# The 47-point part of a transform in front of a feed-forward layer: even and odd sums in six of eight batches

## The chip, the core and the metric

The kernel runs on one core of one Trainium2 chip. The metric is the device time of one execution in microseconds (us); the time before is the median of three runs. A profile of one more execution shows every instruction on the five engines: TensorE (PE, with its weight loads on a line of their own, PEld), VectorE (DVE), ScalarE (ACT), GpSimd (POOL) and SyncE (SP), whose queue issues the transfers (DMA) here.

## The reference

```python
def _attn_ref(x):                      # x: 8 x 3008 x 256, float32
    X = np.fft.fft(x, axis=1)
    X = np.fft.fft(X, axis=2)
    return X.real.astype(np.float32)

def _moe_ref(x, w_in, w_out):          # 24064 tokens, 256 -> 2048 -> 256
    h = x @ w_in
    beta = 1.0
    neg = h <= -beta
    pos = h >= beta
    mid = ~neg & ~pos
    g = np.where(pos, h, np.where(neg, 0.0, (h + beta) ** 2 / (4.0 * beta)))
    return (g @ w_out).astype(np.float32)
```

The real part of a two-dimensional Fourier transform of every batch, and behind it a feed-forward layer over all 8 x 3008 rows of it. The input's layout is changed on the host before the launch and the output's after it; the arithmetic is on the chip.

## The kernel before

**The transform.** 3008 is 64 x 47, so a row number splits into a part of 64 (a) and a part of 47 (b), and the transform along it into a 47-point part (stage 1) and a 64-point part (stage 2). The host sends each element beside the one at the opposite row and column, and the kernel adds the two (`fold_x`, line 137, on POOL): the real part needs no more than this sum. Of the 47 frequencies 24 are computed, since the rest follow by symmetry. The transform along the 256 columns is multiplied into `w_in` once, so the layer's first product takes the rows from stage 2 as they are. One column (number 128, called Nyquist) has a path of its own: a small product (`nyquist`, line 312), a detour of its rows through DRAM, and a term that DVE adds later.

**Stage 1** (`stage1`, line 275) has eight pieces for each batch, one for each tile of 8 x 2 columns. The tile `x` is 128 rows by 2 by 384 values; the first index of 2 is the element and its opposite, and the 384 rows of the product are 8 columns of 47 values, filled up with zeros and cut into three blocks of 128. POOL adds the halves into a tile `y` of 384 columns (line 142; three buffers), which lets the x tile go. PE then multiplies three blocks as weights with a block-diagonal constant of cosines and sines, 144, 192 and 144 columns wide (line 287), all in float32, which takes two instructions for each product. ACT copies the result from the PSUM bank to the tile `z` in four parts of 64 x 192 (line 307). The first piece of a batch also has a difference `yd` (line 148) and one product for the Nyquist column (line 299), with two copies of 64 x 24. All pieces share the one PSUM bank `fft`.

**Stage 2** (`stage2`, line 340) has six pieces of four products of 128 columns (line 350); ACT and DVE split each result into a high and a low half (`pqh`, `pql`).

**The layer.** The work is cut into 384 units: 8 batches, 3 chunks of rows (482, 512 and 512), 16 parts of the 2048 hidden values; batch 0 goes over its chunks twice with 8 parts each. A unit has a first product of 6 PE instructions (`gemm1`, line 396), then DVE's `us` and the two halves of `h` (lines 409, 411, 412), ACT's two steps (417, 418), DVE's larger-of (429, both its inputs in SBUF), ACT's rounding to `gh` (430) and POOL's two low halves `gl` (436), and a second product of 12 PE instructions (`gemm2`, line 448), which runs four units later (`LAG`). Of `uv` there are three PSUM banks, of `h` and `a` three buffers, of `gh` and `gl` four.

**What sets the order.** The start (`LOADS`, `START`) is written out by hand. From there on the program emits, for each unit, its first product, its activation, the weight steps of `STEPS` and the transform pieces due at that unit, and then the second product of the unit four earlier. `PLAN` gives the units of a batch's 15 pieces relative to 48 units before the batch's own, `SECOND_PLAN` those of batch 1. A planner then orders each engine's instructions by readiness in its own simulated time, with program order as priority; the first product of a transform piece is pinned behind what was emitted on PE before it (`pinned`). Within an engine's queue the order is then fixed. Loads of x wait in SP's queue for one of four buffers called `xt`, which the raw weights use too in the first part of the run.

Of the kernel before, what the change touches and what calls it, by code (L numbers as in the profile page):

```python
# [13 lines left out]
ALU = mybir.AluOpType  # L14
# [3 lines left out]

NB, S, D, FF = 8, 3008, 256, 2048
NA, NBB, NC = 64, 47, 24
P = 128
XC = 8
GPC = 4
KT = 3
XW = KT * P
CH = 512
# [12 lines left out]
BM = np.cumsum([0] + [hi - lo for lo, hi in SPANS])  # L41


def _constants():
# [13 lines left out]
    parts = [bm, rm]  # L58
# [59 lines left out]


@with_exitstack  # L120
def fft_ffn_kernel(ctx: ExitStack, tc: tile.TileContext, x, cst, w_in, w_out, out):
    nc = tc.nc

    wts = ctx.enter_context(tc.tile_pool(name="wts", bufs=1))
# [4 lines left out]
    xt, yt, zt, nyb, pq, rows = {}, {}, {}, {}, {}, {}  # L129

    def load_x(b, q):
        tag, bufs = ("xt", 4) if b or q < 4 else ("gl", 4) if q < 7 else ("o", 2)
        t = sb.tile([P, 2, XW], F32, tag=tag, name=f"x_{b}_{q}", bufs=bufs)
        nc.sync.dma_start(t, x[b, q])
        xt[b, q] = t

    def fold_x(b, q):

        t = xt.pop((b, q))
        if b or q:  # L140
            y = sb.tile([P, XW], F32, tag="y", name=f"y_{b}_{q}", bufs=3) if b else t[:, 0]
            nc.gpsimd.tensor_tensor(y, t[:, 0], t[:, 1], op=ALU.add)  # L142
            yt[b, q] = [y]
        else:
            yt[b, q] = [t[:, 0], t[:, 1]]
        if q == 0:
            y = sb.tile([P, NA], F32, tag="yd", name=f"yd_{b}", bufs=1)
            nc.gpsimd.tensor_tensor(y, t[:, 0, :NA], t[:, 1, :NA], op=ALU.subtract)
            yt[b, "d"] = y

    cs = wts.tile([P, _OFF[2]], F32, name="cs")
    nc.sync.dma_start(cs, cst[:, : _OFF[2]])
    bm, rm = (cs[:, _OFF[i] : _OFF[i + 1]] for i in range(2))
    cm = sb.tile([P, _OFF[6] - _OFF[2]], F32, tag="nyb", name="cm", bufs=4)
# [8 lines left out]
    nc.vector.memset(half, 0.5)  # L163

    def load_cm():
        nc.sync.dma_start(cm, cst[:, _OFF[2] :])

    early = [0]

# [98 lines left out]
    def first_delta():  # L268
# [3 lines left out]
            nc.tensor.matmul(pt[:, i], t[:, i * P : (i + 1) * P], half[:1].to_broadcast([1, NA]), start=True, stop=True)  # L272
        nc.scalar.activation(delta[:, :4], pt[:, :, 0], AF.Copy, scale=2.0)

    def stage1(b, q):
        for p in range(q, min(q + 2, XC)):
            if (b, p) in xt and (b, p) not in yt:
                fold_x(b, p)
        if q == 0:
            zt[b] = sb.tile([P, NC, P + 1], F32, tag="z", name=f"z_{b}", bufs=1)  # L280
        z, y = zt[b], yt[b, q]
        bank = fft_bank(b, f"s1_{b}_{q}")
        pt = bank[:, : 8 * 2 * NC]
        for k, (lo, hi) in enumerate(SPANS):
            for j, part in enumerate(y):
                at = k, j
                mm = nc.tensor.matmul(  # L287
                    pt[:, lo:hi],
                    part[:, k * P : (k + 1) * P],
                    bm[:, BM[k] : BM[k + 1]],  # L290
                    start=at == (0, 0),
                    stop=at == (KT - 1, len(y) - 1),
                    skip_group_check=True,
                )
                if at == (0, 0):
                    pinned(b, mm)
        if q == 0:
            pd = bank[:NA, 8 * 2 * NC : 9 * 2 * NC]
            nc.tensor.matmul(pd, yt[b, "d"], bm[:, : 2 * NC], start=True, stop=True)
        for h in range(2):  # L300
            for m in range(2):
                src = pt[h * NA : (h + 1) * NA].rearrange("p (t m c) -> p m c t", t=8, m=2)[:, m]
                dst = z[m * NA : (m + 1) * NA, :, (2 * q + h) * 8 : (2 * q + h + 1) * 8]
                if b == 0 and q in VECTOR_COPIES:
                    nc.vector.tensor_copy(dst, src)
                else:
                    nc.scalar.activation(dst, src, AF.Copy)  # L307
        if q == 0:
            for m in range(2):
                nc.scalar.activation(z[m * NA : (m + 1) * NA, :, P], pd[:, m * NC : (m + 1) * NC], AF.Copy)  # L310

    def nyquist(b):
        pt = fft_bank(b, f"ny_{b}")
# [43 lines left out]
    def pinned(b, matmul):  # L357

        if b:
            tc.keep_in_program_order(matmul)  # L360

    def fft_pieces(b):
        pieces = []
        for q in range(XC):
            pieces.append(lambda q=q: stage1(b, q))
# [126 lines left out]
    def fill(n):  # L492
# [105 lines left out]
```

## Time and profile before

| | |
|---|---|
| median of 3 runs | 1733.8 us (1732.95 to 1735.46) |
| the profiled execution's own time | 1732.59 us |
| its span, first to last instruction | 1730.8 us |
| granted TensorE clock | 0.998 |
| PE busy | 1716.5 us |
| DVE busy | 1383.6 us |
| ACT busy | 1359.8 us |
| POOL busy | 1204.8 us |

Some 1.8 us of the execution lie outside the span. Busy times are sums over the span: an engine that is busy for 99% of it may set the time, one at 70% may still set it somewhere. In the rows of the views an engine, a line of the kernel and an operation come first, then output and inputs by the program's names; `x6` at the end of a row is a count. In the chain and the timeline the first two numbers are the start and the length in us from the span's start, and what stands in brackets at the end is the idle time before and what ended it. Matmuls overlap in their ends, so the time that one adds to a row of them is read from starts, not from its own length.

### The profile page before, as it was taken

What the parts mean: (1) busy time and instruction counts of PE and PEld (TensorE: products, weight loads), DVE (VectorE), ACT (ScalarE), POOL (GpSimd) and SP (SyncE); (2) the same over time, 40 slices, a digit from 0 to 9 for tenths busy, and PEclk for the clock granted to TensorE, in tenths of its full rate; (3) what the DMA queues carried; (4) which work ended last, traced back from release to release, by engine and by line L of the source; (5) the groups of instructions that cost most, each with busy time, mean ns of one, the idle gap of its engine ahead of it and who ended that gap; (6) DMA issues with size and microseconds to landing.
All of it is one profiled execution on the core that took longest, in us unless ns stands there. A gap on an engine that the chain in (4) does not pass through costs nothing.

```text
span 1730.8 us, 21504 instructions
## 1 busy us (share of the span) xinstructions
PE 1716.5 (99%) x7784; PEld 1412.5 (82%) x7784; DVE 1383.6 (80%) x1682; ACT 1359.8 (79%) x1593; POOL 1204.8 (70%) x857
## 2 busy tenths in 40 slices
PE   8999999999999999999999999999999999999999
PEld 5877888888888888888888888888888888888877
DVE  6987888777888777877788878887788787888887
ACT  6888877888778887778877887778877788777776
POOL 3767876777667776677757686667866666766775
PEclk9999999999999999999999999999999999999999
DMA  6123220111001110010100111001100001000000
GB/s 232 36 71 123 102 77 25 46 32 62 1 25 51 37 53 20 5 60 29 52 25 10 51 37 43 25 10 57 47 28 26 9 24 43 1 25 24 1 25 25
DMA packets 33456, 72.44 MB, mean 42 GB/s; under 512 B 4547, under 2 KB 9667, under 8 KB 33350
## 3 DMA queue, kind: packets, MB, share of 16 engines
q1 hardware_dynamic: 33350, 71.07, 12.2%
q8 instruction: 61, 1.00, 0.2%
q14 instruction: 45, 0.37, 0.1%
HBM read 43.25 MB, written 27.81 MB: 41 GB/s over the span
## 4 chain that ended last, share of the span: by engine, by line
PE 92%; ACT 2%; POOL 2%; DVE 2%; issue 1%; DMA 1%; ACTq 0%; POOLq 0%
PE acc L468 57%; PE uv L400 29%; PE s L287 3%; PE s L350 2%; POOL gl L436 2%; DVE h L429 1%; ACT gh L430 1%; ACT a L418 1%; ACT a L417 0%; PE wps L249 0%; DMA nyr<-nyt 0%; PE warm L494 0%; DMA nyb<-nyr 0%; ACT z L307 0%; DVE h L412 0%
## 5 line engine op out<-in xcount | busy, mean ns | idle before, releaser
L436 POOL TENSOR_TENSOR gl<-h,gh 128x512 fp32r<-128x512 f32 (+1 forms) x765 | 1100.7, 1462 | 483.0 <-ACT gh L430 433.2
L429 DVE SCALAR_TENSOR_TENSOR h<-a,h 128x1024 f32<-128x1024 f32 (+1 forms) x385 | 560.9, 1458 | 184.1 <-ACT a L418 182.4
L430 ACT ACTIVATE gh<-h 128x1024 fp32r<-128x1024 f32 (+1 forms) x385 | 401.0, 1042 | 317.6 <-DVE h L429 267.0
L468 PE MATMUL acc<-gh,woh 128*128 128x512 f32 (+1 forms) x1536 | 611.3, 398 | 1.6 <-ACT gh L430 1.6
L468 PE MATMUL acc<-gl,woh 128*128 128x512 f32 (+1 forms) x1536 | 602.7, 392 | 0.5 <-POOL gl L436 0.4
L468 PE MATMUL acc<-gh,wol 128*128 128x512 f32 (+1 forms) x1536 | 601.8, 392 | 0.0
L417 ACT ACTIVATE a<-h,half 128x1024 f32<-128x1024 f32 (+1 forms) x385 | 431.8, 1122 | 15.9 <-DVE h L412 13.6
L418 ACT ACTIVATE a<-a 128x1024 f32<-128x1024 f32 (+1 forms) x385 | 399.0, 1037 | 7.7
L468 PEld LDWEIGHTS acc<-gl,woh 128*128 128x128 f32 x1536 | 289.7, 189 | 64.5 <-POOL gl L436 2.1
L468 PEld LDWEIGHTS acc<-gh,woh 128*128 128x128 f32 x1536 | 290.1, 189 | 61.9 <-ACT gh L430 1.8
L409 DVE SCALAR_TENSOR_TENSOR us<-nyb,delta,uv 128x512 f32<-128x512 f32 (+1 forms) x384 | 280.4, 730 | 74.8 <-PE uv L400 72.6
L468 PEld LDWEIGHTS acc<-gh,wol 128*128 128x128 f32 x1536 | 290.1, 189 | 59.0 <-issue 0.7
L411 DVE TENSOR_TENSOR h<-us,uv 128x512 f32<-128x512 f32 (+1 forms) x384 | 259.6, 676 | 56.4 <-POOL gl L436 16.3
L400 PE MATMUL uv<-pqh,wh 128*128 128x512 f32 (+1 forms) x768 | 301.7, 393 | 1.3 <-DVE us L409 0.6
L400 PE MATMUL uv<-pql,wh 128*128 128x512 f32 (+1 forms) x768 | 301.2, 392 | 0.0
L400 PE MATMUL uv<-pqh,wl 128*128 128x512 f32 (+1 forms) x768 | 300.7, 392 | 0.0
L412 DVE TENSOR_TENSOR h<-us,uv 128x512 f32<-128x512 f32 (+1 forms) x384 | 256.4, 668 | 0.0
L400 PEld LDWEIGHTS uv<-pqh,wh 128*128 128x128 f32 x768 | 144.9, 189 | 35.0 <-DVE wl L179 1.2
L400 PEld LDWEIGHTS uv<-pqh,wl 128*128 128x128 f32 x768 | 145.0, 189 | 31.4 <-issue 0.5
L400 PEld LDWEIGHTS uv<-pql,wh 128*128 128x128 f32 x768 | 145.0, 189 | 31.4 <-DVE pql L179 0.4
L307 ACT ACTIVATE z<-s 64x192 f32<-64x192 f32 x244 | 82.6, 339 | 7.4 <-PE s L287 2.2
L142 POOL TENSOR_TENSOR y<-x 128x384 f32<-128x384 f32 x56 | 80.0, 1429 | 4.6 <-DMA x<-in_x_dram 3.9
(56 smaller groups left out, 495.3 us busy)
## 6 DMA issues: line engine op xcount, KB each, us to landing
x<-in_x_dram SPq DMA_DIRECT2D x64, 384.0 KB, 3.0
out_dram<-o SPq DMA_DIRECT2D x30, 512.0 KB, 3.1
out_dram<-o SPq DMA_DIRECT2D x16, 482.0 KB, 3.2
nyb<-nyr SPq DMA_DIRECT2D x23, 256.0 KB, 5.5
raw<-in_moe_w_in_dram SPq DMA_DIRECT2D x8, 512.0 KB, 5.0
raw<-in_moe_w_out_dram SPq DMA_DIRECT2D x8, 512.0 KB, 6.4
part<-o SPq DMA_DIRECT2D x4, 512.0 KB
o<-part SPq DMA_DIRECT2D x4, 512.0 KB
```

The costliest lines, as they stand in the source:

```text
L142: nc.gpsimd.tensor_tensor(y, t[:, 0], t[:, 1], op=ALU.add)
L307: nc.scalar.activation(dst, src, AF.Copy)
L400: nc.tensor.matmul(t[:, :n], w[m][:, cols], r[:, m, :n], start=(j == 0), stop=(j == 2))
L409: nc.vector.scalar_tensor_tensor(us, nyb[b, k][:, :n], delta[:, f : f + 1], uv[0], op0=ALU.mult, op1=ALU.add)
L411: nc.vector.tensor_tensor(h[:, 0], us, uv[1], op=ALU.subtract)
L412: nc.vector.tensor_tensor(h[:, 1], us, uv[1], op=ALU.add)
L417: nc.scalar.activation(a[:, sl], h[:, sl], AF.Relu, bias=half, scale=0.5)
L418: nc.scalar.activation(a[:, sl], a[:, sl], AF.Square)
L429: nc.vector.scalar_tensor_tensor(h[:, sl], a[:, sl], 1.0, h[:, sl], op0=ALU.min, op1=ALU.max)
L430: nc.scalar.activation(gh[:, sl], h[:, sl], AF.Copy)
L436: eng.tensor_tensor(gl[:, sg], h[:, sg], gh[:, sg].bitcast(F32), op=ALU.subtract)
L468: nc.tensor.matmul(acc[:, :n], w[:, f, wc], g[:, sg], start=(first and j == 0), stop=(last and j == 2))
```

## The change

Batches 2 to 7 (`N_DENSE = 2`) get another stage 1, `stage1_even_odd`; batches 0 and 1 keep theirs. Cosine is even in b and sine is odd, so the sum of the values at b and -b goes to the cosines and the difference to the sines, each with 24 rows instead of 47. Five columns of 24 rows make 120 rows for one product, and the product is 120 columns wide. A tile now has 2 x 5 x 2 = 20 columns of x, so that six tiles hold 120 of the columns and a seventh, half as long, holds the rest with the Nyquist column among them; it comes second in `ORDER`. A full piece has four products, the half one two, 26 in a batch. The separate difference and product for the Nyquist column fall away. ACT copies 64 x 240 four times for a full piece, and 64 x 120 and 64 x 96 for the half one.

POOL makes the sums in the x tile itself (`fold_even_odd`): one operation over 512 columns and two over 256 for a full tile; over 256, 128, 128 and 128 for the half one, the second of these on 24 rows. So a tile stays in its `xt` buffer until its products have run. In batch 1 `fold_x` also writes in place; the three `y` buffers go. The x tiles of batches 2 to 7 are 120 rows of 4096 bytes where they were 128 rows of 3072.

The units of the pieces are new in `PLAN` (14 pieces) and `SECOND_PLAN` (15). The constants of the new products are one more load at the end of `LOADS`.

```diff
-G_ORDER = np.arange(P).reshape(XC, GPC, 2, 2).transpose(0, 3, 1, 2).reshape(-1)
+N_DENSE = 2
+ORDER = (0, 6, 1, 2, 3, 4, 5)
...
+    ang = 2 * np.pi * (np.outer(b[:HB], C_ORDER) % NBB) / NBB
+    pm = np.concatenate([np.kron(np.eye(GJ), f(ang)) for f in (np.cos, np.sin)], axis=1)
...
-LOADS = "l0 x0 l1 m0 x1 x2 x3 x4 x5 x6 x7 l4 l5 l2 l3 l6 l7"
+LOADS = "l0 x0 l1 m0 x1 x2 x3 x4 x5 x6 x7 l4 l5 l2 l3 l6 l7 j0"
...
-PLAN = [14, 17, 20, 22, 25, 28, 31, 33, 35, 36, 41, 48, 52, 56, 59]
-SECOND_PLAN = [26, 28, 30, 32, 34, 36, 38, 40, 41, 42, 44, 48, 52, 56, 59]
+PLAN = [13, 18, 19, 21, 24, 28, 30, 35, 36, 38, 46, 52, 57, 58]
+SECOND_PLAN = [24, 27, 28, 32, 34, 36, 38, 40, 42, 44, 44, 46, 53, 53, 57]
...
     def load_x(b, q):
         tag, bufs = ("xt", 4) if b or q < 4 else ("gl", 4) if q < 7 else ("o", 2)
-        t = sb.tile([P, 2, XW], F32, tag=tag, name=f"x_{b}_{q}", bufs=bufs)
-        nc.sync.dma_start(t, x[b, q])
+        if b >= N_DENSE:
+            n = 2 if q < XE - 1 else 1
+            t = sb.tile([KR, 2, 4, P], F32, tag=tag, name=f"x_{b}_{q}", bufs=bufs)[:, :n]
+            nc.sync.dma_start(t, xe[b - N_DENSE, q, :, :n])
...
         if b or q:
-            y = sb.tile([P, XW], F32, tag="y", name=f"y_{b}_{q}", bufs=3) if b else t[:, 0]
+            y = t[:, 0]
             nc.gpsimd.tensor_tensor(y, t[:, 0], t[:, 1], op=ALU.add)
...
+    def fold_even_odd(b, q):
+
+        t = xt[b, q]
+        pair = t.rearrange("p r (k two) x -> p two (r k) x", two=2)
+        n = KR if q < XE - 1 else KR - HB
+        nc.gpsimd.tensor_tensor(pair[:n, 0], pair[:n, 0], pair[:n, 1], op=ALU.add)
+        if n < KR:
+            nyq = pair[n:, :, :, :NA]
+            nc.gpsimd.tensor_tensor(nyq[:, 0], nyq[:, 0], nyq[:, 1], op=ALU.subtract)
+        nc.gpsimd.tensor_tensor(t[:, :, 1], t[:, :, 0], t[:, :, 2], op=ALU.add)
+        nc.gpsimd.tensor_tensor(t[:, :, 3], t[:, :, 0], t[:, :, 2], op=ALU.subtract)
...
+    def stage1_even_odd(b, n):
+        for m in range(n, min(n + 2, XE)):
+            if (b, ORDER[m]) not in folded:
+                folded.add((b, ORDER[m]))
+                fold_even_odd(b, ORDER[m])
+        if n == 0:
+            new_z(b)
+        q = ORDER[n]
+        z, t = zt[b], xt.pop((b, q))
+        rs = t.shape[1]
+        pt = fft_bank(b, f"s1_{b}_{q}")[:, : 2 * rs * KR].rearrange("p (m r x) -> p m r x", m=2, r=rs)
+        for r in range(rs):
+            for m in range(2):
+                mm = nc.tensor.matmul(pt[:, m, r], t[:, r, 2 * m + 1], pm[:, m], start=True, stop=True)
+                if r + m == 0:
+                    pinned(b, mm)
+        for h in range(2):
+            cols = rs * GJ
+            first = 20 * q + cols * h
+            if rs == 1:
+                cols, first = (4, 120) if h else (5, 124)
+            for m in range(2):
+                src = pt[h * NA : (h + 1) * NA, m].rearrange("p r (j c) -> p c (r j)", j=GJ)[:, :, :cols]
+                nc.scalar.activation(z[m * NA : (m + 1) * NA, :, first : first + cols], src, AF.Copy)
...
-            if n + 4 < XC:
-                plan[i].append(lambda b=b, q=n + 4: load_x(b, q))
+            if n + 4 < len(order(b)):
+                plan[i].append(lambda b=b, q=order(b)[n + 4]: load_x(b, q))
```

More of the change, by code (lines that the diff above doesn't have):

```diff
@@ L14 @@
 ALU = mybir.AluOpType
-NB, S, D, FF = 8, 3008, 256, 2048
+NB = 8
+S, D, FF = 3008, 256, 2048
 NA, NBB, NC = 64, 47, 24
@@ L24 @@
 XC = 8
-GPC = 4
+XE = 7
+HB = 24
+GJ = 5
+KR = GJ * HB
 KT = 3
@@ L35, with _slots @@
 WIDTH = [7 * NA + 34, CH, CH]
-G_ORDER = np.arange(P).reshape(XC, GPC, 2, 2).transpose(0, 3, 1, 2).reshape(-1)
+N_DENSE = 2
+ORDER = (0, 6, 1, 2, 3, 4, 5)
 SPANS = [(k * P // NBB * 2 * NC, (min((k + 1) * P, 8 * NBB) - 1) // NBB * 2 * NC + 2 * NC) for k in range(KT)]
 BM = np.cumsum([0] + [hi - lo for lo, hi in SPANS])
+def _slots():
+    table = np.full((XE, 2, 2, GJ), -1)
+    table[: XE - 1] = np.arange(120).reshape(XE - 1, 2, 2, GJ).transpose(0, 2, 1, 3)
+    table[XE - 1, 0, 1, :4] = np.arange(120, 124)
+    table[XE - 1, 0, 0, :4] = np.arange(124, 128)
+    table[XE - 1, 0, 0, 4] = 0
+    return table
 def _constants():
@@ L120, in fft_ffn_kernel @@
 @with_exitstack
-def fft_ffn_kernel(ctx: ExitStack, tc: tile.TileContext, x, cst, w_in, w_out, out):
+def fft_ffn_kernel(ctx: ExitStack, tc: tile.TileContext, x, xe, cst, w_in, w_out, out):
     nc = tc.nc
@@ L127, in fft_ffn_kernel @@
     ps = ctx.enter_context(tc.tile_pool(name="ps", bufs=1, space=bass.MemoryType.PSUM))
-    xt, yt, zt, nyb, pq, rows = {}, {}, {}, {}, {}, {}
+    xt, yt, zt, nyb, pq, rows, folded = {}, {}, {}, {}, {}, {}, set()
     def load_x(b, q):
         tag, bufs = ("xt", 4) if b or q < 4 else ("gl", 4) if q < 7 else ("o", 2)
-        t = sb.tile([P, 2, XW], F32, tag=tag, name=f"x_{b}_{q}", bufs=bufs)
-        nc.sync.dma_start(t, x[b, q])
+        if b >= N_DENSE:
+            n = 2 if q < XE - 1 else 1
+            t = sb.tile([KR, 2, 4, P], F32, tag=tag, name=f"x_{b}_{q}", bufs=bufs)[:, :n]
+            nc.sync.dma_start(t, xe[b - N_DENSE, q, :, :n])
+        else:
+            t = sb.tile([P, 2, XW], F32, tag=tag, name=f"x_{b}_{q}", bufs=bufs)
+            nc.sync.dma_start(t, x[b, q])
         xt[b, q] = t
@@ L139, in fold_x @@
         t = xt.pop((b, q))
+        if q == 0:
+            y = sb.tile([P, NA], F32, tag="yd", name=f"yd_{b}", bufs=1)
+            nc.gpsimd.tensor_tensor(y, t[:, 0, :NA], t[:, 1, :NA], op=ALU.subtract)
+            yt[b, "d"] = y
         if b or q:
-            y = sb.tile([P, XW], F32, tag="y", name=f"y_{b}_{q}", bufs=3) if b else t[:, 0]
+            y = t[:, 0]
             nc.gpsimd.tensor_tensor(y, t[:, 0], t[:, 1], op=ALU.add)
@@ L145, in fold_x @@
             yt[b, q] = [t[:, 0], t[:, 1]]
[L146 to L152, printed above, removed]
+    def fold_even_odd(b, q):
[8 more added lines that the diff above has]
+        nc.gpsimd.tensor_tensor(t[:, :, 3], t[:, :, 0], t[:, :, 2], op=ALU.subtract)
+    cs = wts.tile([P, _OFF[3]], F32, name="cs")
+    nc.sync.dma_start(cs[:, : _OFF[2]], cst[:, : _OFF[2]])
     bm, rm = (cs[:, _OFF[i] : _OFF[i + 1]] for i in range(2))
-    cm = sb.tile([P, _OFF[6] - _OFF[2]], F32, tag="nyb", name="cm", bufs=4)
+    pm = cs[:KR, _OFF[2] :].rearrange("p (m x) -> p m x", m=2)
+    cm = sb.tile([P, _OFF[7] - _OFF[3]], F32, tag="nyb", name="cm", bufs=4)
     mats = [[cm[:, (2 * m + h) * P : (2 * m + h + 1) * P] for h in range(2)] for m in range(2)]
@@ L165, in load_cm, with load_pm @@
     def load_cm():
[L166 removed]
+        nc.sync.dma_start(cm, cst[:, _OFF[3] :])
+    def load_pm():
+        nc.sync.dma_start(cs[:, _OFF[2] :], cst[:, _OFF[2] : _OFF[3]])
     early = [0]
@@ L273, in first_delta, with new_z @@
         nc.scalar.activation(delta[:, :4], pt[:, :, 0], AF.Copy, scale=2.0)
+    def new_z(b):
+        zt[b] = sb.tile([P, NC, P + 1], F32, tag="z", name=f"z_{b}", bufs=1)
     def stage1(b, q):
@@ L360, in pinned, with order @@
             tc.keep_in_program_order(matmul)
+    def order(b):
+        return range(XC) if b < N_DENSE else ORDER
     def fft_pieces(b):
         pieces = []
-        for q in range(XC):
-            pieces.append(lambda q=q: stage1(b, q))
+        stage = stage1 if b < N_DENSE else stage1_even_odd
+        for q in range(XC if b < N_DENSE else XE):
+            pieces.append(lambda q=q: stage(b, q))
         pieces.append(lambda: nyquist(b))
@@ L567 @@
     xs = np.stack([xs[:, n][..., g], xs[:, neg][..., np.where(g == 0, P, D - g)]])
-    xs = xs.reshape(2, NB, NA, NBB, XC, 2 * GPC, 2).transpose(1, 4, 5, 3, 0, 6, 2)
-    xp = np.zeros((NB, XC, KT * P, 2, P), xs.dtype)
-    xp[:, :, : 8 * NBB] = xs.reshape(NB, XC, 8 * NBB, 2, P)
-    xp = np.ascontiguousarray(xp.reshape(NB, XC, KT, P, 2, P).transpose(0, 1, 3, 4, 2, 5))
+    dense = xs[:, :N_DENSE].reshape(2, N_DENSE, NA, NBB, XC, 2, 8).transpose(1, 4, 6, 3, 0, 5, 2)
+    xp = np.zeros((N_DENSE, XC, KT * P, 2, P), xs.dtype)
+    xp[:, :, : 8 * NBB] = dense.reshape(N_DENSE, XC, 8 * NBB, 2, P)
+    xp = np.ascontiguousarray(xp.reshape(N_DENSE, XC, KT, P, 2, P).transpose(0, 1, 3, 4, 2, 5))
+    slots = _slots()
+    used = (slots >= 0)[:, :, :, :, None, None]
+    xe = np.zeros((NB - N_DENSE, XE, GJ, HB, 2, 4, 2, NA), xs.dtype)
+    for k in range(4):
+        bs = np.arange(HB) if k < 2 else (NBB - np.arange(HB)) % NBB
+        part = np.where(used, xs[k % 2, N_DENSE:].transpose(0, 3, 2, 1)[:, slots][..., bs, :], 0)
+        if k >= 2:
+            part[..., 0, :] = 0
+        xe[:, :, :, :, :, k] = part.transpose(0, 1, 4, 5, 2, 3, 6)
     arrays = {
-        "x": xp.reshape(NB, XC, P, 2, XW),
+        "x": xp.reshape(N_DENSE, XC, P, 2, XW),
+        "xe": xe.reshape(NB - N_DENSE, XE, KR, 2, 4, P),
         "cst": _CONST,
```

12 lines of the change are left out of this document (7 added, 5 removed).

## The prediction

> **What bounds the kernel now.** I read the page's busy times first, then the stretch in which one batch does its stage 1 beside the stretch behind it, then the chain.
>
> ```profile
> span 1730.8 us, 21504 instructions
> PE 1716.5 (99%) x7784; PEld 1412.5 (82%) x7784; DVE 1383.6 (80%) x1682; ACT 1359.8 (79%) x1593; POOL 1204.8 (70%) x857
> ```
>
> ```profile
> 518.00:610.00 92.00, 92.00 (x421) 76.54 (x421) 72.65 (x85) 75.66 (x98) 70.26 (x51) 1.00 0.13 41
> 610.00:720.00 110.00, 110.00 (x504) 91.00 (x503) 87.97 (x109) 85.00 (x91) 72.27 (x51) 1.00 0.09 31
> ```
>
> The second fence gives length, then busy time of PE, PEld, DVE, ACT and POOL. Stage 1 of a batch lies between 518 and 610. PE has no free time in either stretch, so a microsecond of PE work taken out is a microsecond of time, as long as no other engine then makes PE wait. POOL is at 76% in the first stretch and 66% in the second.
>
> ```profile
> 605.63 1.40 PE uv L400 x6
> 607.03 0.81 PE s L287 x6
> 607.85 2.79 PE acc L468 x12
> 610.64 1.40 PE uv L400 x6
> 612.04 2.80 PE acc L468 x12
> ...
> 616.49 3.00 PE acc L468 x12
> 619.48 1.40 PE uv L400 x6
> 620.88 0.89 PE s L350 x8
> 621.77 2.82 PE acc L468 x12
> 624.59 1.40 PE uv L400 x6
> ```
>
> ```profile
> 520.84 1.31 PE uv L400 x6
> ...
> 522.97 0.24 PE s L299 x2
> ...
> 526.06 1.32 PE uv L400 x6
> 527.38 2.64 PE acc L468 x12
> ```
>
> The chain is PE alone. A quiet unit takes 1.40 + 2.80 = 4.20 us; the one with a stage-1 piece 610.64 - 605.63 = 5.01, so the piece costs 0.81; a stage-2 piece of eight instructions costs 0.89. The first piece of a batch: 526.06 - 520.84 = 5.22 against 1.32 + 2.64 = 3.96 for a quiet unit of 482 columns, so 1.26.
>
> **The change on PE.** It removes in each of six batches 7 x 0.81 + 1.26 = 6.93 us. What it adds are 52 instructions of 120 columns with weights of 128 columns. By columns: a dense piece streams 2 x 480 columns in 0.81 us, 0.84 ns each, so 120 columns would take 0.101 us. But there is a floor:
>
> ```profile
> 21.39 1.89 PE L328 MATMUL nys<-cs,z 128*128 128x64 f32 x16
> 16.18 1.10 PE L272 MATMUL dps<-half,drow 1*128 1x64 f32 x8
> L328 PE MATMUL nys<-cs,z 128*128 128x64 f32 x16 | 1.9, 272 | 0.0
> ```
>
> Sixteen instructions of only 64 columns, each with new weights of 128, take (1.89 - 0.27) / 15 = 0.108 us each, twice what their columns need, and the eight with a single row of weights are no quicker. Stage 2 has 0.89 / 8 = 0.111. So the weights set the pace below about 128 columns, whatever the rows, and I take 0.111 for the new instruction: a full piece costs what a stage-2 piece costs, 0.89, the half one 0.89 - 4 x 0.111 = 0.45. Six and a half pieces: 6 x 0.89 + 0.45 = 5.79. The saving is 6.93 - 5.79 = 1.14 a batch, **6.8 us in six batches**. Bounds: at 0.101 the 52 instructions are 0.5 us shorter in a batch, 3 us in all, so 9.8; the other end is the second rival. (The Trainium skill, "TensorE: Matmul & The Clock Gate", section "LDWEIGHTS (loading the stationary operand)", has a weight load last the columns of the weights divided by 1.2 GHz, 107 ns for 128, whatever the rows. That speaks against narrower products as a saving. The rows above agree within 4%; by its figure the saving would be some 1.3 us larger, an estimate from that page.)
>
> **The change on POOL.** This is the step that decides.
>
> ```profile
> L436 POOL TENSOR_TENSOR gl<-h,gh 128x512 fp32r<-128x512 f32 x509 | 752.7, 1502 | 307.6 <-ACT gh L430 278.4 <-PE acc L468 15.3 <-PE s L350 4.6
> L142 POOL TENSOR_TENSOR y<-x 128x384 f32<-128x384 f32 x56 | 80.0, 1429 | 4.6 <-DMA x<-in_x_dram 3.9 <-PE s L287 0.7
> ```
>
> ```profile
> 569.04 1.30 POOL L436 TENSOR_TENSOR gl<-h,gh 128x512 fp32r<-128x512 f32 x1
> 602.31 1.03 POOL L142 TENSOR_TENSOR y<-x 128x384 f32<-128x384 f32 x1
> 603.29 6.26 POOL L436 TENSOR_TENSOR gl<-h,gh 128x512 fp32r<-128x512 f32 x4
> 609.51 1.99 POOL L142 TENSOR_TENSOR y<-x 128x384 f32<-128x384 f32 x1
> ```
>
> ```profile
> 598.37 0.69 DVE L411 TENSOR_TENSOR h<-us,uv 128x512 f32<-128x512 f32 x1
> ...
> 602.17 0.75 DVE L409 SCALAR_TENSOR_TENSOR us<-nyb,delta,uv 128x512 f32<-128x512 f32 x1 [0.37 <-PE uv L400]
> ...
> 604.53 1.23 DVE L429 SCALAR_TENSOR_TENSOR h<-a,h 128x1024 f32<-128x1024 f32 x1 [0.78 <-ACT a L418]
> ...
> 609.09 1.54 DVE L429 SCALAR_TENSOR_TENSOR h<-a,h 128x1024 f32<-128x1024 f32 x1 [0.55 <-ACT a L418]
> ```
>
> ```profile
> 128.47 0.33 POOL L148 TENSOR_TENSOR yd<-x 128x64 f32<-128x64 f32 x1
> ...
> 136.59 1.02 POOL L142 TENSOR_TENSOR y<-x 128x384 f32<-128x384 f32 x1 [3.33 <-DMA x<-in_x_dram]
> 137.57 3.54 POOL L436 TENSOR_TENSOR gl<-h,gh 128x512 fp32r<-128x512 f32 x2
> ```
>
> Alone, POOL takes 1.30 us for 512 columns, 1.03 for 384 and 0.33 for 64. The same sum takes 1.99 when it starts at 609.51 while DVE's line 429 runs (609.09 to 610.63): POOL ends 0.87 after DVE does, as if it had hardly begun before. At 604.53 DVE takes 1.23, and 1.54 at 609.09, where it began before the low half of the x4 row had ended (609.55). So these two kinds of work take turns.
>
> Between 64 and 384 columns the slope is 0.70 / 320 us, so 256 columns cost 0.75 and 128 cost 0.47. A full tile: 1.30 + 2 x 0.75 = 2.8; the half one 0.75 + 3 x 0.47 = 2.2; a batch 19 us. Before: 8 x 1.03 + 0.33 = 8.6. So POOL has 10.4 us more work in a batch, in the same stretch. In a quiet unit the turns need 2 x 1.30 + 1.23 = 3.8 of 4.20 us by the rows, some 3.6 if neighbours overlap by about 0.05 at each end as 602.31 + 1.03 and 603.29 do. From unit 18 to 30 there are 12 units and six pieces: 12 x 4.20 + 6 x 0.89 = 55.7 us. Needed are 12 x 3.6 to 3.8, 43 to 46, and five full tiles and the half one, 16.2: 59 to 62. The turns fall short by 4 to 6.
>
> What covers it: the unit whose `h` DVE began at 598.37 has its low halves done at 609.55, the end of the x4 row. The buffer of `h` is wanted three units after 598.37, 13.4 us later with one piece between, at 611.8: 2.2 us spare. After that DVE is late, and PE waits only when a bank of `uv` isn't read: the one read by 602.92 is wanted by the second half of the next first product, at 605.63 + 0.70 = 606.3: 3.4 us spare. Together 5.6. The second product, which wants these low halves at about 617.0 (third instruction behind 616.49), has 7.4. So a shortfall of 4 to 6 just fits or misses by a little. I take a stall of **0.2 us a batch, 1.2 us in all**, between 0 and the first rival; the nearer row is the spare 5.6. What POOL already costs is small:
>
> ```profile
> DVE h L411 <- POOL gl L436: 16.3, 24, 1.8
> x<-in_x_dram SPq DMA_DIRECT2D x64, 384.0 KB, 3.0
> L307 ACT ACTIVATE z<-s 64x192 f32<-64x192 f32 x244 | 82.6, 339 | 7.4 <-PE s L287 2.2 <-PE s L299 1.8
> ```
>
> **Beside other work.** ACT's copies: 32 of 339 ns and two small ones become 24 longer ones and four short; the columns copied stay, ten starts become fewer, ACT is not in the chain: nothing. Transfers: 6.5 tiles of 480 KB for 8 of 384, the same bytes; a load now waits for PE's products, not for POOL's sum, and lands about 3 us after its issue, three pieces ahead of its use. Behind it in SP's queue stand the Nyquist rows (unit 35, five units behind the last piece) and the stores of `o`, which have 16 units. The load of constants is wanted 60 units later. All nothing, as long as POOL doesn't reach a sum before its load.
>
> **The start.** In batch 1 the x tiles hold `xt` buffers that the last weights want too, and pieces move.
>
> ```profile
> PE s L287 <- DVE raw L226: 2.7, 2, 2.4
> raw<-in_moe_w_out_dram SPq DMA_DIRECT2D x8, 512.0 KB, 6.4
> ```
>
> A piece now waits 2.7 us for the shared bank: at best that goes. At worst a weight load comes late by one transfer, 6.4. I take 0, the nearer end.
>
> **Sum.** -6.8 + 1.2 + 0 = -5.6. The profiled execution took 1732.6 us (span 1730.8 and 1.8 around it), so 1727.0; the median of the runs shown is 1.2 higher, so **1728.2** for a run.
>
> **Rivals.**
>
> *POOL too late (slower).* The row at 136.59 shows the pattern that sums in place make regular: a buffer comes free, is loaded, and POOL waits 3.33 us for the load with two low halves behind it (137.57). The planner put the sum there too early. If that happens before the cluster at units 18, 19 and 21, the shortfall of 4 to 6 grows to 7.3 to 9.3; less the spare 5.6, PE stalls 1.7 to 3.7 us a batch. With 2.8: 6 x 2.8 - 6.8 = +10, **1743.8**. It decides from 1.14 us a batch, where the saving is gone. For it: the queues are fixed in advance, and POOL is full there. Against it: PE has no stall now with sums in the same stretch, and POOL that is already late finds the load landed. (The Trainium skill, "SBUF — State Buffer", section "Who interferes with whom", calls this an exclusive lock: a GpSimd operation that reads SBUF and a VectorE one with two SBUF inputs exclude each other. The rows 609.09 and 609.51 agree.)
>
> *Other weights, other pace (slower).* A change of the weights' shape costs PE time: the Nyquist pair (64 columns of weights) makes the first piece 1.26 - 0.81 = 0.45 longer, 0.23 more than two instructions at 0.111. If 120 rows for 128 count as such a change, 7 x 0.23 x 6 = 9.7 us: -6.8 + 9.7 + 1.2 = +4.1, **1737.9**. Against it: the single-row weights keep the pace among themselves; what they cost at their edges is the doubt.
>
> *Columns, not weights.* The new instruction takes 0.101: **1725.2**.
>
> *Nothing to see.* Half a microsecond more stall a batch, or the start 3 us later: about **1731.5**.
>
> **How the numbers follow.** Forecast 0.52, own range 1724 to 1730; columns 0.06; nothing to see 0.17; POOL too late 0.18; other pace 0.07. A measurement of this kernel tells about 0.2% from no change, 3.5 us: faster below 1730.3, slower above 1737.3. So faster 0.52 + 0.06 = 0.58, same 0.17, slower 0.25. The range goes from 1722 (columns, and the wait of 2.7 gone) to 1742, short of the POOL rival's middle, which leaves out some 0.15.
>
> **What would show it.** Right: the chain after unit 60 is PE alone, pieces of 8 at 0.89 and of 4 at 0.45, units with a full piece at 5.09, POOL near 87% in the stretch of stage 1. Wrong: eight instructions in 0.81 (columns) or over 1.0 (pace); idle time of PE ended by DVE or POOL between units 18 and 31; POOL's new sums with idle time ended by the x load. The first unit of batch 2 that comes earlier or later than before by a microsecond or more would show the term for the start wrong.

## The result, and the profile after

The changed kernel takes 1747.3 us (median of 6 runs, 1746.8 to 1750.3) beside 1735.3 for the kernel before on the same chip: 1.0075 of it, 95% interval 1.0062 to 1.0088. It is 0.75% slower, and the interval lies clear of 1; 1728.2 was forecast, and the range ended at 1742.

The page of the changed kernel, its head and the shares of the chain, and then the shares of the chain before:

```profile
span 1745.2 us, 21636 instructions
PE 1713.4 (98%) x7796; PEld 1401.0 (80%) x7796; DVE 1391.1 (80%) x1682; ACT 1354.9 (78%) x1557; POOL 1281.7 (73%) x935
PE 71%; POOL 12%; ACT 7%; DVE 5%; issue 4%; DMA 0%; ACTq 0%; POOLq 0%; DVEq 0%
```

```profile
PE 92%; ACT 2%; POOL 2%; DVE 2%; issue 1%; DMA 1%; ACTq 0%; POOLq 0%
```

PE is busy for 3.1 us less than before, yet the span is 14.4 longer. In the chain POOL, ACT and DVE had 6% together before, and none where the prediction looked; now they have 24%. The next two fences give one stretch of stage 1, before and then after (length, then busy PE, PEld, DVE, ACT, POOL):

```profile
728.00:826.00 98.00, 98.00 (x448) 81.43 (x447) 75.76 (x88) 80.11 (x103) 72.15 (x52) 1.00 0.13 41
```

```profile
728.00:826.00 98.00, 96.41 (x446) 79.19 (x445) 73.32 (x85) 76.44 (x94) 83.67 (x63) 1.00 0.16 43
```

POOL has 11.5 us more to do (it is busy for 85% of the stretch; near 87% was forecast), and PE has 1.6 us of idle time where it had none. The granted clock is 1.00 in both.

Where the 14.4 us come from is read from the chain, by the first products of units 60 and 300. Before, then after:

```profile
302.44 1.32 PE uv L400 x6
...
1355.06 1.32 PE uv L400 x6
```

```profile
299.79 1.32 PE uv L470 x6
...
1367.94 1.32 PE uv L470 x6
```

Unit 60 comes 2.65 us earlier, unit 300 12.9 us later: 15.5 lost in five batches. The sixth, in which the last transform is made, loses 0.6; the last batch, without any transform beside it, 1.1; the rest gains 0.2. Together -2.65 + 15.5 + 0.6 + 1.1 - 0.2 = 14.4. If PE saves 1.14 a batch, as the next rows bear out, what PE loses to waits beside the transforms is 15.5 + 0.6 + 6.8 = 23 us. The largest of PE's waits in the whole execution, with the total, the number of times and the longest:

```profile
PE s L366 <- ACT z L376: 8.1, 6, 1.7
PE s L416 <- ACT nyt L383: 4.2, 5, 1.2
PE uv L470 <- DVE us L479: 4.0, 5, 0.9
```

From the second of the six batches on they stand at two places in a batch.

**Place A, units 18 and 19.** The chain there (units are counted as in `PLAN`; batch 4):

```profile
752.04 0.44 PE s L366 x4
752.48 2.65 PE acc L538 x12
755.13 0.72 PE uv L470 x3
755.85 0.27 ACT z L376
...
756.67 0.76 ACT a L487
...
757.73 0.27 ACT z L376
...
758.04 1.15 PE s L366 x8
759.19 2.65 PE acc L538 x12
761.84 1.39 PE uv L470 x6
...
767.43 0.89 PE s L366 x8
768.31 2.80 PE acc L538 x12
```

The half piece takes 0.44 and a full piece 0.89; 0.45 and 0.89 were forecast. But the piece at 19 wants the bank of the piece at 18, and that bank is emptied only at 758.0, though its product ended at 752.5. ACT's own order shows why:

```profile
752.61 1.07 ACT L500 ACTIVATE gh<-h 128x1024 fp32r<-128x1024 f32 x1 [1.56 <-DVE h L499]
753.58 1.14 ACT L487 ACTIVATE a<-h,half 128x1024 f32<-128x1024 f32 x1
754.75 1.06 ACT L488 ACTIVATE a<-a 128x1024 f32<-128x1024 f32 x1
755.83 0.84 ACT L376 ACTIVATE z<-s 64x120 f32<-64x120 f32 x3
```

The copies stand behind a `gh` for which ACT had to wait 1.56 us, because DVE was late. A step of 4.93 (4.04 and a full piece) becomes 6.67 to 6.87 in five of six batches.

**Place B, units 33 to 36,** the chain from the sum to PE's stall:

```profile
819.98 1.25 POOL x L178
...
822.01 0.75 POOL x L183
822.75 3.50 POOL gl L506 x2
...
826.28 0.69 DVE h L481
...
827.57 2.28 DVE h L499
...
829.95 1.06 ACT gh L500
...
831.99 1.47 DVE h L499
...
833.57 1.06 ACT gh L500
834.63 1.05 ACT a L487
...
836.78 0.22 ACT nyt L383
...
837.05 1.16 PE s L416 x8
```

A sum delays two low halves, these hold a buffer of `h` from DVE, DVE's larger-of collides with POOL (2.28), ACT gets `h` late, and its copy of the Nyquist rows, which empties the bank `fft` for stage 2, comes last. Ahead of that, at unit 35, PE has waited 0.90 us for DVE's `us`, so for a bank of `uv`: here the layer's own path makes PE wait too. Units 35 and 36 take 5.80 + 6.25 us in place of 4.64 + 5.10, units 32 to 34 some 0.3 more than before.

**How early the sums run.** If the first sums of the 42 tiles and the 42 pieces are matched in order, the sum at 819.98 is that of the fourth tile of batch 5, and its product starts at 981.6, 162 us later. From batch 3 on, three tiles of each batch are summed 41 to 42 us ahead of their product, and four 160 to 180 us ahead, beside the transform of the batch before. (In the kernel before, three tiles of eight were as early, by 142 to 149 us.) The sixth batch has no such tiles of a next one, and it has no wait at place B. From the fifth on, each sum starts 5 to 12 us behind the piece four places earlier, whose products free one of the four `xt` buffers for the load, so the units of the pieces set the places of the sums too. POOL's queue therefore puts work that could wait ahead of low halves that can't. No run here holds the sums back by themselves, so what that would win is open.

### The profile page after: what moved, and what is told of

Its sections match the earlier page's. It is cut to its first block, busy times and chain, and to the rows that moved or that the text cites. A ratio compares the mean times of both kernels' runs of the same rounds, so it can differ in the third digit from the quotient of the medians.

```text
span 1745.2 us, 21636 instructions
## 1 busy us (share of the span) xinstructions
PE 1713.4 (98%) x7796; PEld 1401.0 (80%) x7796; DVE 1391.1 (80%) x1682; ACT 1354.9 (78%) x1557; POOL 1281.7 (73%) x935
## 4 chain that ended last, share of the span: by engine, by line
PE 71%; POOL 12%; ACT 7%; DVE 5%; issue 4%; DMA 0%; ACTq 0%; POOLq 0%; DVEq 0%
PE acc L538 44%; PE uv L470 22%; POOL gl L506 10%; DVE h L499 3%; PE s L416 2%; ACT gh L500 2%; ACT a L488 2%; PE s L366 2%; ACT a L487 2%; POOL x L178 2%; POOL x L183 1%; DVE h L481 0%; DVE h L482 0%; ACT z L376 0%; PE wps L287 0%
## 5 line engine op out<-in xcount | busy, mean ns | idle before, releaser
L499 DVE SCALAR_TENSOR_TENSOR h<-a,h 128x1024 f32<-128x1024 f32 (+1 forms) x385 | 576.0, 1497 | 216.4 <-ACT a L488 215.2
L178 POOL TENSOR_TENSOR x<-x 120x512 f32<-120x512 f32 (+1 forms) x42 | 72.3, 1722 | 3.2 <-DMA x<-in_xe_dram 3.1
L376 ACT ACTIVATE z<-s 64x240 f32<-64x240 f32 (+2 forms) x168 | 61.3, 365 | 2.6
```

The costliest lines, as they stand in the source:

```text
L178: nc.gpsimd.tensor_tensor(pair[:n, 0], pair[:n, 0], pair[:n, 1], op=ALU.add)
L376: nc.scalar.activation(z[m * NA : (m + 1) * NA, :, first : first + cols], src, AF.Copy)
L499: nc.vector.scalar_tensor_tensor(h[:, sl], a[:, sl], 1.0, h[:, sl], op0=ALU.min, op1=ALU.max)
```

## The experiments

The table is worked out from the starts of the first products in each trace. "Batch" is the mean of the three batches between units 156 and 300. "Waits" is that time less 210.55 - 1.14 = 209.41 us, the batch of the kernel before with PE's saving; for the kernel before and the one built on it, less 210.55.

```
kernel                     us      ratio [95%]               batch    waits
before                   1733.8                              210.55    0
after                    1747.3   1.0075 [1.0062, 1.0088]    214.04    4.6
e1  piece 18 to 17       1745.2   1.0066 [1.0051, 1.0081]    213.70    4.3
e2  35, 36, 38 later     1755.0   1.0122 [1.0107, 1.0137]    215.44    6.0
e3  both                 1752.3   1.0104 [1.0087, 1.0121]    214.91    5.5
e4  two sums left out    1725.1   0.9952 [0.9937, 0.9967]    210.06    0.7
e5  memsets for sums     1740.9   1.0037 [1.0025, 1.0050]    213.27    3.9
e6  two sums on DVE      1794.1   1.0341 [1.0326, 1.0357]    221.17   11.8
e7  spread               1758.8   1.0138 [1.0123, 1.0153]    214.93    5.5
e8  spread, on DVE       1812.9   1.0453 [1.0437, 1.0468]    223.80   14.4
e9  clear of 20 and 36   1754.6   1.0124 [1.0107, 1.0141]    214.69    5.3
e10 old units            1733.8   1.0004 [0.9995, 1.0013]    210.00    0.6
e11 before, more sums    1765.6   1.0182 [1.0164, 1.0200]    215.78    5.2
e12 two units earlier    1744.5   1.0064 [1.0051, 1.0078]    212.89    3.5
e13 old units but start  1730.2   0.9976 [0.9966, 0.9986]    210.26    0.9
e14 one unit later       1751.0   1.0097 [1.0081, 1.0112]    214.47    5.1
e15 after, less 1 sum    1745.4   1.0068 [1.0053, 1.0083]    213.75    4.3
e16 e14, less 1 sum      1749.9   1.0089 [1.0073, 1.0106]    214.22    4.8
```

**Are A and B two faults of the places, or one of lateness?**

```diff
-PLAN = [13, 18, 19, 21, 24, 28, 30, 35, 36, 38, 46, 52, 57, 58]
+PLAN = [13, 17, 19, 21, 24, 28, 30, 35, 36, 38, 46, 52, 57, 58]   # e1
+PLAN = [13, 18, 19, 21, 24, 28, 30, 39, 41, 43, 46, 52, 57, 58]   # e2
+PLAN = [13, 17, 19, 21, 24, 28, 30, 39, 41, 43, 46, 52, 57, 58]   # e3
```

> The changed kernel, with one stage-1 piece of batches 2 to 7 moved from unit 18 to 17, so that no two stage-1 pieces stand in neighbouring units. Two theories on the 4.7 us that PE now stands still per batch. Bank: the stall at unit 19 (6.7 us for 5.0) is the piece waiting until ACT has emptied the one shared bank of the piece at 18; then it goes, 1.75 us in each of six batches, 10.5 in all, so 1747.3 - 10.5 = 1736.8, and the stall at units 33 to 36 stays. POOL: ACT is late only because POOL's new sums hold up the low halves; then the same lateness meets the next piece, and no more than 4 us are won (1743 or more).

> The changed kernel, with the Nyquist piece and the first two stage-2 pieces of batches 2 to 7 moved from units 35, 36, 38 to 39, 41, 43. The neighbours 18 and 19 stay. POOL: the backlog that starts with the sums after the pieces at 28 and 30 has gone by unit 38, where DVE is 1.0 us late after 4.3 at unit 35; so the 2.3 us at units 35 and 36 go in five batches, 11.5 in all: about 1736. The 0.5 us at units 32 to 34 stay. Bank: the Nyquist piece and the stage-2 piece are no neighbours any more, the same 1736; but if it is the POOL backlog itself that PE has to wait for, the stall turns up at units 33 to 36 all the same, now ended by DVE, and little is won (1743 or more).

> Both moves of the two kernels before in one. If the two stalls are independent, both gains add: 1747.3 - 10.5 - 11.5 = 1725, some 10 us below the kernel before, of which 6.8 would be PE's shorter stage 1 and the rest the earlier start of batch 1. If the stalls are one shortage of POOL's that shows wherever a piece meets it, clearly less: 1733 to 1740.

In e1 the stall at 19 is gone, but unit 20, where the second product starts a new chunk, takes 5.2 in place of 4.2; 1.0 of 1.75 us only moves. In e2 units 35 and 36 have no piece any more and take 5.37 + 6.67 = 12.04 us; with the pieces it was 12.05. So the pieces were not what PE waited for there: behind the late layer they ran for nothing, and elsewhere they cost 0.44 + 0.89 a batch again. What PE waits for in e2 is the accumulators, which ACT empties behind the same ring:

```profile
839.77 1.54 DVE h L499
...
841.39 1.06 ACT gh L500
842.45 0.49 ACT o L549
...
842.99 0.96 PE acc L538 x3
```

One lateness meets whichever result PE wants next. In e3 the two gains should have added to 1725; it took 1752.3. The theory of two independent places falls.

**Do POOL's new sums make it late?** In e4 the two sums over 256 columns are left out. In e5 each is replaced by three memsets, which write to the same places and read nothing. In e6 both are made by DVE. In e11 the kernel before gets two more sums behind each x tile; in a batch's first tile they overwrite what the Nyquist difference reads afterwards (the expectation says that nothing reads it), so that column changes.

```diff
-        nc.gpsimd.tensor_tensor(t[:, :, 1], t[:, :, 0], t[:, :, 2], op=ALU.add)
-        nc.gpsimd.tensor_tensor(t[:, :, 3], t[:, :, 0], t[:, :, 2], op=ALU.subtract)
+        for _ in range(3): nc.gpsimd.memset(t[:, :, 1], 0.0)      # e5; none in e4
+        for _ in range(3): nc.gpsimd.memset(t[:, :, 3], 0.0)
...
-                mm = nc.tensor.matmul(pt[:, m, r], t[:, r, 2 * m + 1], pm[:, m], start=True, stop=True)
+                mm = nc.tensor.matmul(pt[:, m, r], t[:, r, 2 * m], pm[:, m], start=True, stop=True)   # e4, e5
...
+        nc.vector.tensor_tensor(t[:, :, 1], t[:, :, 0], t[:, :, 2], op=ALU.add)        # e6
+        nc.vector.tensor_tensor(t[:, :, 3], t[:, :, 0], t[:, :, 2], op=ALU.subtract)
...
+            if b > 1:                                             # e11, in before's fold_x
+                for _ in range(2):
+                    nc.gpsimd.tensor_tensor(t[:, 1, :256], t[:, 0, :256], t[:, 1, :256], op=ALU.add)
```

> The changed kernel without the last two of POOL's sums on each tile of batches 2 to 7 (the even and the odd sum are left out, and the products read the tile's two halves as they stand, so the transform of these batches is not computed); units, products, copies and loads as they are. POOL has 1.5 us less for a full tile. POOL: the stall at units 32 to 36 goes (2.6 us in five batches, 13 in all), and the one at unit 19 goes or shrinks: 1724 to 1734. Bank and units alone: the stalls at units 19 and 35 to 36 stay as they are, about 1746.

> The changed kernel with the last two sums on each tile of batches 2 to 7 left out, as in the kernel without them, and in their place on POOL three memsets each, of about the same length together (a memset of 512 columns took 0.52 us before), which write SBUF but read nothing. The transform of these batches is not computed. So POOL is as busy as in the changed kernel, but takes no turns with DVE's line 429 in that time. POOL's own time is what is short: the stalls stay, 1742 to 1748. The turns with DVE are what is short: as without the sums, 1725 to 1729.

> The changed kernel with the last two sums on each tile of batches 2 to 7 on DVE instead of POOL; all is computed. POOL's work is that of the kernel without these sums, which took 1725.1; DVE gets 12 operations of 256 columns and two of 128 in a batch, some 0.4 us each by its 0.68 us for 512, 5 us in 200. POOL's time short: 1725 to 1730, faster than before. The turns short: a third of the gain is lost, since a sum on DVE takes its turn too, if shorter: 1730 to 1738. If DVE becomes the bound, over 1740.

> The kernel before, with its 47-point part as it was; POOL makes two more sums over 256 columns behind each sum of an x tile of batches 2 to 7, into the half of the tile that nothing reads any more. That is 8 x 2 x 0.75 = 12 us more of POOL's time in a batch, where the change adds 10.4, and nothing else is changed. If POOL's time alone sets the loss, each batch loses 3 to 6 us in units 16 to 36: 18 to 36 us in all, 1752 to 1770 us. If it takes the sums in place, ACT's longer copies or the new units, the batches lose under 1 us each: 1732 to 1740 us.

In e4 and e5 POOL's first sums stand behind the same low halves as in the changed kernel, in all batches, so its order is not what differs. Without the two sums the waits fall from 4.6 to 0.7 a batch and the kernel is at 1725.1, within 2 us of what PE's saving and the start give. So at these units the sums are needed for the loss. Three memsets follow each other by 0.25 us, 0.76 together, where a free sum takes 0.74; they keep 3.9 of 4.6, and 1740.9 us is just below the range for POOL's own time:

```profile
L183 POOL MEMSET x<- 120x256 f32 x108 | 33.7, 312 | 1.8
L185 POOL MEMSET x<- 120x256 f32 x108 | 33.7, 312 | 0.1
```

None of these memsets took over 0.32 us, so they took no turns. POOL's own time is the larger share; what the turns of these two sums with DVE add is (214.04 - 213.27) / (214.04 - 210.06), a fifth. e11 comes from the other side: two more sums, in the old kernel at its old units, cost 5.2 a batch (by their free time they are 12 us, where the change adds 10.4). So such a loss needs neither ACT's longer copies, nor products that read the x tile, nor the new units.

DVE, with time to spare by its busy share, is no place for them. The waits of e6:

```profile
DVE x L182 <- POOL x L178: 75.1, 35, 4.3
DVE x L182 <- POOL x L181: 19.0, 5, 3.8
```

DVE's sum waits in its queue for POOL's first one, up to 4.3 us, with the layer's `us` and `h` behind it. My expectation of a gain was wrong.

**Does more room help?** e7 spreads the pieces, e9 keeps them clear of the places where a chunk starts (20 and 36), e10 goes back to the old units in all batches, e13 in batches 2 to 7 alone. e12 and e14 keep the old spacing and shift it.

```diff
+PLAN = [5, 9, 13, 21, 25, 29, 35, 38, 40, 42, 44, 46, 48, 50]       # e7, e8
+PLAN = [5, 8, 11, 14, 22, 25, 28, 31, 38, 40, 42, 44, 46, 48]       # e9
+SECOND_PLAN = [24, 27, 28, 32, 34, 36, 38, 40, 42, 44, 44, 46, 48, 50, 51]   # e7, e8, e9
+PLAN = [14, 17, 20, 22, 25, 28, 31, 35, 36, 41, 48, 52, 56, 59]     # e10, e13
+SECOND_PLAN = [26, 28, 30, 32, 34, 36, 38, 40, 41, 42, 44, 48, 52, 56, 59]   # e10
+PLAN = [12, 15, 18, 20, 23, 26, 29, 35, 36, 41, 48, 52, 56, 59]     # e12
+PLAN = [15, 18, 21, 23, 26, 29, 32, 35, 36, 41, 48, 52, 56, 59]     # e14
```

> The changed kernel, all computed, with stage 1's seven pieces of batches 2 to 7 spread out: units 5, 9, 13, 21, 25, 29, 35, then the Nyquist piece at 38 and stage 2 at 40, 42, 44, 46, 48, 50; for that, batch 1's last three pieces at 48, 50, 51 for 53, 53, 57. POOL's work is the same. If its shortage is one of bunching (seven tiles within 17 units), the sums now have four units each, 1.6 to 2.4 us of free turns and 0.9 from the piece, against 2.8: nearly no stall, 1725 to 1731. If POOL is short over the whole batch, 1740 or more.

> The changed kernel with all its sums; only the pieces' units are others: stage 1 at 5, 8, 11, 14, 22, 25, 28, the Nyquist product at 31, stage 2 at 38 to 48, and the last pieces of batch 1 at 48, 50, 51. No piece stands within two units ahead of the places where the second product starts a new chunk (units 20 and 36), and the sums lie over 24 units in place of 12. One shortage of POOL, which only costs where POOL has no time to make it up: 24 units give about 24 x 0.5 + 6 x 0.89 = 17 us for 19 us of sums, so nearly all fits: 0 to 1 us of stall a batch, no unit over 0.5 above its quiet step but one at 20 or 36, 1724 to 1731 us. Any lateness meets the accumulators' emptying at a new chunk, wherever the pieces are (as with the spread units before): a step of over 1.5 us too much at 20 or 36 in each batch, 1738 to 1750 us.

> The changed kernel with all its sums at the units of the kernel before: stage 1 at 14, 17, 20, 22, 25, 28, 31, the Nyquist product at 35, stage 2 at 36, 41, 48, 52, 56, 59, and batch 1 at its old units. If POOL's added sums set the loss: stalls of 3 to 5 us a batch again, at 32 to 36 above all, 1741 to 1752 us. If the new units are to blame and not the sums: no stall, 1727 to 1732 us. For the start: if the units of batch 1 gave the 2.65 us by which unit 60 came earlier, unit 60 is back at the time that it has in the kernel before, to within 0.7 us; if the sums in place or the x tiles gave it, it stays 2 us or more earlier.

> The changed kernel with all its sums; the spacing of the pieces is that of the kernel before, but stage 1 of batches 2 to 7 stands two units earlier: 12, 15, 18, 20, 23, 26, 29, the Nyquist product and stage 2 at the units of the kernel before (35, 36, 41, 48, 52, 56, 59), batch 1 at the changed kernel's units. With the old units the low halves of a unit end 10.3 us after its first product at unit 35 (9.7 in the kernel before), and only unit 36 is too long, by 0.6 to 0.9 us. If lateness of POOL is made up by some 0.3 us a unit once the sums have ended: two units more give 0.6 us, the stall at 36 goes, and each batch keeps its 1.14 us: 1727 to 1731 us. If lateness isn't made up ahead of unit 36, whatever lies between: a stall of 0.6 to 0.9 us or more at 36 in each batch, 1732 to 1740 us.

> The changed kernel with all its sums; batches 2 to 7 at the units of the kernel before (14, 17, 20, 22, 25, 28, 31, 35, 36, 41, 48, 52, 56, 59), batch 1 at the changed kernel's units. With both plans old unit 60 came 0.6 us earlier than in the kernel before, with the new units of batch 1 2.4 to 2.7 us. If the units of batch 1 give that gain by themselves, unit 60 comes 2.2 to 2.8 us earlier here, the rest goes as with both plans old, and the time is 1731 to 1733 us. If the gain at the start is given back (an order of the queues that follows from it), the batches behind lose other amounts than with both plans old (0.3 to 0.8 us gained in each but the first): 1734 us or more.

> As the kernel with the old units in batches 2 to 7, but its stage 1 one unit later: 15, 18, 21, 23, 26, 29, 32; batch 1 at the changed kernel's units. Two units earlier cost some 11 us, though the spacing was the same. If the loss grows with the units between the sums and the new chunk at unit 36 (lateness stays and is added to): one unit later loses less than the old units, 1728 to 1732 us. If the last sums just before unit 36 set it: units 35 and 36 together over 1.5 us too long in each batch, 1736 to 1744 us. If it is only the order that the planner happens to make in each queue, neither follows, and the stalls stand at other units.

(The 10.3 and 9.7 us in the expectation of e12 were counted to low halves one and a half units too early; rightly it is 17.7 and 17.1. The difference stands.) e8 is e7 with DVE's sums; 1724 to 1727 us was expected, and it took 1812.9, as e6 had gone. e9, e10 and e12 fell outside both of their ranges, so the ideas in their expectations hold in part at best.

Spreading makes it worse. In e7 unit 36 takes 8.4 us for 4.2. Some 2.5 of the difference are a wait, since the copies of the piece at 35 and a step of the layer stand on ACT ahead of the accumulators:

```profile
PEld acc L538 <- ACT a L487: 17.0, 6, 2.9
PE acc L538 <- ACT a L487: 14.6, 6, 2.5
```

The other 1.8 are the clock: behind the wait the second product takes 4.59 us for 2.80, and the granted clock is 0.66 from 841 to 846 us, where it is 1.00 in the 5 us before and the 4 us after. So a part of e7's loss is not POOL's. (Over the whole span e6, e7 and e8 have 0.992, 0.994 and 0.989; the changed kernel has 1.0.)

In e9, with no piece near, unit 36 still takes 6.7, and units 27 to 33 lose another 2.3. In POOL's queue the tiles of e7 and e9 stand at least three units' low halves apart from batch 3 on, those of e13 once only two. So the idea that room between the sums makes up for them falls too. But at the old units the same sums cost only 0.6 (e10) and 0.9 (e13) in the middle batches, all of it at unit 36, though 3.9 and 2.2 in the first of the six. e13 is the fastest kernel here that computes everything, 0.24% below the kernel before, with an interval clear of 1. That old units alone are no safeguard is shown by e11. The stretch of e13:

```profile
728.00:826.00 98.00, 98.00 (x455) 81.03 (x454) 77.26 (x90) 79.74 (x97) 89.42 (x65) 1.00 0.15 43
```

POOL is at 91%, more than in the changed kernel (85%); its first sums take longer, as they do when they collide with DVE's larger-of. The groups of both kernels, after and then e13:

```profile
L178 POOL TENSOR_TENSOR x<-x 120x512 f32<-120x512 f32 x36 | 62.0, 1721 | 3.2 <-DMA x<-in_xe_dram 3.1
L182 POOL TENSOR_TENSOR x<-x 120x256 f32<-120x256 f32 x36 | 32.8, 911 | 2.4
```

```profile
L178 POOL TENSOR_TENSOR x<-x 120x512 f32<-120x512 f32 x36 | 73.9, 2053 | 7.6 <-DMA x<-in_xe_dram 7.6
L182 POOL TENSOR_TENSOR x<-x 120x256 f32<-120x256 f32 x36 | 33.6, 934 | 2.7
```

And yet PE has no idle time in it. One unit later (e14) or two earlier (e12) the waits are 5.1 and 3.5. How near the edge this is shows in the end of a unit's second low half, counted from the start of its first product (worked out from the traces, batch 4):

```
unit     25    26    27    28    29    30    31    32    33    34
before  14.7  15.6  14.9  15.5  16.4  16.8  15.2  16.9  15.3  15.2
e13     15.9  16.7  15.4  18.4  17.0  15.4  18.5  17.0  15.4  16.1
after   15.6  17.3  16.0  19.0  17.9  19.9  17.3  19.0  17.2  17.6
e14     18.4  17.1  16.9  19.0  20.2  17.5  19.2  20.8  18.0  18.7
```

PE wants the low halves 4 x 4.20 + 1.40 + 0.47 = 18.7 us after the first product, and 0.89 later for each piece between. A sum adds some 2 to 3 us. In e13 the units behind a sum bring it back to about 15.4 before the next; in the others it is not brought back as far.

For the start, e13's profiled execution lost 2.1 us more than the changed kernel's in its first 12 units, before any piece, and was 2.0 above its median; from unit 24 to 60 it gains 3.26 on the kernel before, the changed kernel 3.27, and e10 with the old units of batch 1 only 1.03. So some 2.2 us of the start's gain are the units of batch 1; the rest is not taken apart.

**Is it one operation's place in the queue?** In the eight kernels with both sums on POOL, in the changed form, that lose much, the half tile's last operation stands one unit behind its others; in e10 and e13 it stands with them. e15 and e16 leave it out.

```diff
+        if n == KR:
             nc.gpsimd.tensor_tensor(t[:, :, 3], t[:, :, 0], t[:, :, 2], op=ALU.subtract)
```

> The changed kernel without one small operation for each batch: the difference over 128 columns of the half tile (0.63 us by its row) is left out, so the sine part of its columns isn't the reference's; all else and all units are as in the changed kernel. In all eight kernels that lost 10 us or more in batches 2 to 7 this operation stands behind the low halves of one more unit than the half tile's other sums, in the two that lost nothing it stands with them. If that place sets off the loss: most of the 3.5 us a batch goes, 1728 to 1735 us. If it is only a sign of it: 0.5 us of POOL in a batch, so at most 3 us in all, 1743 to 1747 us.

> The same operation left out, in the kernel whose stage 1 stands one unit later than in the kernel before (it took 1751 us). If the place of that operation sets off the loss: 1730 to 1738 us. If it is only a sign: 1747 to 1751 us.

Both lose what they lost before, within 0.3 us a batch. The place was a sign and not the cause.

**What stays open.** The same sums with the same spacing cost 0.9, 5.1 or 3.5 us a batch at three places a unit or two apart. The orders of POOL, DVE and ACT are fixed for each by the planner, and I found no single place in them that decides. That lateness is kept in the ring of POOL, DVE and ACT is read from the chains; why it is brought back at the old units is not shown. Nor is it shown what the same sums would cost at the same units if POOL made them later, nearer to their products.

## Why the prediction was wrong

**PE's saving: right.** A full piece takes 0.89, a half one 0.44, a unit with a full piece 5.09. The sixth batch of e10 and e13, in which PE has no wait, takes 209.39 us for 210.49 before: 1.10 less, where 1.14 was forecast. The rivals "columns" and "other pace" are out.

**POOL's durations: right, with a gap.** Free sums took 1.27 to 1.30, 0.74 and 0.46 us where 1.30, 0.75 and 0.47 were forecast. The means are higher by the turns, 1.72 and 0.91, and the half tile's first sum, 0.75 by the forecast, took 1.72 to 1.74 each time. (The Trainium skill, "SBUF — State Buffer", section "Who interferes with whom", has a POOL operation that reads SBUF and a DVE one with two SBUF inputs exclude each other at a shared port; the first sum's 1.27 at least and 2.32 at most in this trace agree.) The shortage of 4 to 6 us was not measured by itself. Its sum counts the half piece as a full one and units 18 and 19 as 4.20 us, though they take 4.04; rightly it is 0.8 larger. That it is near the 4.6 lost is no proof of it, since e13 has the same sums, POOL busier, and loses 0.9.

**The step that failed: "a shortfall of 4 to 6 just fits", a stall of 0.2 us a batch.** Measured were 4.6 in the middle batches, 23 us in all six. The spare of 5.6 was counted along the layer's own path, from the low halves through `h` to the banks of `uv`. Even there it did not last: at unit 35 PE waits 0.90 us for a bank of `uv` in four batches. The larger part was never in the sum: ACT, which gets `h` late, has in the same queue the copies of the bank `fft`, those of the Nyquist rows and the emptying of the accumulators, and PE waits for these much sooner: at unit 19 ACT's 1.56 us of lateness became 1.75 of PE at once. For those results no spare was worked out. Nor did the working ask when the sums are wanted: four of the seven tiles summed in such a stretch belong to the next batch. I also took POOL's spare time in quiet units as paying the debt back; e9 has quiet units enough and still loses.

**ACT's copies "nothing", and no term for the new units: wrong.** The copies are what ended PE's wait at place A, since two pieces stand in neighbouring units and share one bank. And without the new units most of the loss is gone: with the old ones it is 0.6 to 0.9 in the middle batches. Without the sums, at the new units, it is 0.7. So it takes both, the sums and the places.

**Transfers: right.** A load of x landed 4.4 us after its issue where 3 was taken, but POOL waited only 3.1 us in all for these loads. So the rival "POOL too late", whose 2.8 us a batch and 1743.8 came nearest, had the engine right, but the load that was to make it late hardly did; its number came near by another way.

**The start: 0 taken, -2.65 measured,** all but the best of the bounds; some 2.2 us of it come from the units of batch 1. The last batch's 1.1 had no term either: its unit 36 takes 5.64 us in place of 4.51 even in e4, so the two sums do not cause it.

With the measured terms the sum is -6.8 + 23.0 - 2.65 + 1.1 - 0.2 = +14.4, the difference of the spans; the 23.0 was taken from that difference, so the sum shows the sizes and proves nothing.

## What to carry to other kernels

Where engines with fixed queues work in a ring, the spare of an added operation is the smallest one over every result that stands behind a late instruction in any queue, not that along the path it belongs to: list what else the late engine owes, and when it is wanted. Ask too when the added operation's own result is wanted: here most sums ran 40 to 180 us early, ahead of work that was due. A planned order is part of the cost of a change: price the change at the old places first, and the new places as an edit of their own. POOL at 91% cost 0.9 us a batch and at 85% 4.6, so the busy share doesn't price such an edit.

## What I had not expected

Two low halves that collide with DVE's larger-of take 3.50 us, and the larger-of 2.28 where 1.23 is its free time: both sides pay. The Nyquist and the first stage-2 piece ran wholly inside a stall, so that moving them out of it cost their full 0.44 + 0.89 us a batch. And a memset of 256 columns on POOL takes 0.31 us where a sum takes 0.74, so it was three of them, 0.25 us apart, that stood in for a sum.
